# A decode block and its gradients: two more pools of big tiles, one at each end of SBUF, in place of an early, hurried middle of batch 1

## The chip, the core and the metric

The kernel runs on one NeuronCore of a Trainium2 chip. The metric is the device time of one execution in microseconds (us): before, 941.38 us, the median of three runs (940.76 to 941.86). The profile is of one execution whose span, from the first to the last instruction, is 938.9 us.

The engines are TensorE (PE in the profile, with its weight loads, PEld, apart), VectorE (DVE), ScalarE (ACT), GpSimd (POOL) and SyncE (SP). SP issues the loads, GpSimd the stores of the big gradients, ScalarE those of the weight gradients.

## The reference

One step of attention with a cache of keys and values, then a small ReLU network, and the gradients of all inputs:

```python
B, Sq, D = 2, 1, 640
H, Sk, Dh, Dff = 32, 4096, 128, 1728
q = layernorm(x) @ wq                        # B x H heads of 128
p = softmax(q . K * Dh**-0.5)                # K: [2, 32, 4096, 128] bf16
h = x + (p . V) @ wo                         # V: the same shape
h2 = h + relu(layernorm(h) @ w1) @ w2
out_0 = h2
out_1 .. out_7 = gradients for x, K, V, wq, wo, w1, w2 from grad_out
```

K and V of one head are 4096 x 128 bf16, 1 MB each; there are 64 pairs (batch, head). The gradients of K and V are as large as K and V and are outer products: for each head gV = p (x) go, and gK = gs (x) q, where go is the gradient of the head's output and gs = p * (V . go - p . (V . go)). So go has to be known first, and it needs the gradient that comes back through the network, w1 and wo: that is what the kernel calls the middle of a batch.

## The kernel before

**Pass one** walks over the 64 pairs: it loads K and V, transposes K, makes the scores, e = exp, the products K*e, and with them M = V^T (K*e) and the head's output. M (`MT`, one tile of 128 x 128 for each head) gives the gradient for q later, without a further pass over K. **Pass two** walks over the 64 pairs again, which it calls turns: it loads V once more (`W`), transposes it, makes V . go, and writes gV and gK. Turns 0 to 12 are laid between the iterations of pass one for batch 1; the others run by themselves when pass one has ended.

Between them lies the **middle** of a batch: wo, layer norm, w1, ReLU, the way back through w1, and go for each head by dot products of VectorE with rows of wo (`ttr`). It is a generator in the background queue `bg`. Three background queues are stepped, each by its own credit:

```python
def turn():                       # a dot product waits for a slot
    while slot[0] <= 0:
        yield 0.0
    slot[0] -= 1

def wait(n):                      # steps until another engine's result is due
    end = step[0] + n * spread[0]
    while step[0] < end and not forced[0]:
        yield 0.0
    yield

def middle_gen(b):
    ...                           # wo, layer norm, w1, ReLU
    for k in range(3):
        for c in range(ND):
            yield from turn()
            ttr(w1_t[:, c, k * FW:(k + 1) * FW], fbc[:, k * FW:(k + 1) * FW], gx2p[:, c, k:k + 1], FW)
            yield 0.85
    yield ("w1", b)
    ...                           # layer norm backward
    for h0, h1 in bounds:         # the kept heads first, then groups of 8
        yield from go_group(b, h0, h1, hbc)    # a ttr with wo for each head, then M's part; marks ("go", b, h)
```

**The big tiles.** K, V, W, the results gK and gV, the weights that are streamed, and the strips of the weight gradients share 12 tiles of 8 KB a partition (32 x 128 bf16). Each tile has a home under a tag: `ld` for loads, `g` for gK and gV, `f` for strips, `q` for weights late in the kernel. `take` gets a free tile of a tag, `give` returns it, and `share` says how many each tag ought to own; a tile moves over when it comes free. A tile that was handed on is written only when its last reader is done, and for gK and gV that is the store.

```python
NBIG = 12
homes = {"ld": list(range(NBIG)), "g": [], "f": [], "q": []}
def goes_to(tag):
    if owned[tag] > wanted.get(tag, NBIG):
        for other in homes:
            if owned[other] < wanted.get(other, 0):
                return other
    return tag
def more_home(tag, pool):
    homes[tag].append(len(pools)); pools.append(pool)
    free[tag] += 1; owned[tag] += 1
```

**Kept heads.** The V tiles of the last 6 heads of batch 0 and the last 5 of batch 1 are not given back after pass one, and are not loaded again. The order of the turns is

```python
KEPT = (6, 5)
turns = [(b, h) for b in range(B) for h in (*range(H - KEPT[b], H), *range(H - KEPT[b]))]
KEPT1_AT = 22
turns[KEPT1_AT:H + KEPT[1]] = turns[H:H + KEPT[1]] + turns[KEPT1_AT:H]
```

so the kept heads of batch 1 are turns 22 to 26, ahead of the last ten heads of batch 0.

**One turn of pass two** (half a tile is 128 x 2048; the lines L438, L451, L822 and so on of the profile are in these helpers):

```python
def p2_iter(j, busy):             # c = turn j, p = turn j - 1
    pair_matvec(p["dp"], p.pop("T3"), 3, gom[:, hp, bp, :, :])
    nc.vector.scalar_tensor_tensor(out=gsp[:], ...)          # gs of the turn before
    ...                                                      # go and q spread over the partitions, p in pairs
    c["T0"] = pair_transpose(c["W"], 0)
    gK = take("g", ...); outer_half(gK, p["rb"][:, 128:256], gsp, 0)
    yield
    outer_half(gK, p["rb"][:, 128:256], gsp, 1)
    nc.gpsimd.dma_start(out=natural(out_2, bp, hp), in_=gK[:]); give(gK)
    yield
    ...                                                      # T1; T2, with V . go of the quarters before
    c["T3"] = pair_transpose(c["W"], 3)
    give(c["W"], "g" if j < H and owned["g"] < 3 else None)
    gV = take("g", ...); outer_half(gV, c["rb"][:, 0:128], c["pp"], 0)
    yield
    outer_half(gV, c["rb"][:, 0:128], c["pp"], 1)
    nc.gpsimd.dma_start(out=natural(out_3, b, h), in_=gV[:]); give(gV)
    yield
```

**The late parts.** When w1 of batch 1 has been used, its memory is released and becomes a pool `fin` and one more big tile `big2`, of the tag `f`. `fin_gen` then makes the gradients of w2, w1, wo and wq (14.9 MB in 18 strips) with outer products of two rows on TensorE, copied from PSUM mostly by ScalarE; `outer_rows` takes a tile `f` for each strip once it has rested 13 steps. When every go is known, `gx_gen` loads wq again, transposes it and makes the gradient of x, and `mlp_out` makes h2 with w2.

The loop over the turns, after pass one:

```python
if i is None and plan[n - 1][0] is not None:     # the first turn that is alone
    share(ld=KEPT[1] + 3, g=4)
if fin is not None and not bg2 and not bg3:
    share(ld=7, g=6)
elif fin is not None and j >= KEPT1_AT + KEPT[1] - 1:
    share(ld=4, g=4, f=3, q=2)
...
if i is None:
    spread[0] = 2 if ("w1", B - 1) in done else 1
    hurry = ("go", *turns[KEPT1_AT]) not in done
    k = 0
    while g2 is not None:                        # seven steps a turn
        p2_step(); pump()
        slot[0] = int(k in ((0, 1, 3, 4, 5) if hurry else (1, 4)))
        k += 1
        bg_step(0, rate); bg_step(1, RATE2); bg_step(2, RATE3)
```

`pump` issues the next loads as long as a tile `ld` is free. `bg_until` forces the middle on if a turn's go isn't there yet.

Of the kernel before, what the change touches and what calls it, by code (L numbers as in the profile page):

```python
# [15 lines left out]
def kernel(  # L16
# [79 lines left out]

    def goes_to(tag):

        if owned[tag] > wanted.get(tag, NBIG):
            for other in homes:  # L100
                if owned[other] < wanted.get(other, 0):
                    return other
        return tag
# [218 lines left out]
    nc.vector.tensor_copy(out=gc[:].rearrange("p c b -> p b c"), in_=xg32[:, B:2 * B, :])  # L322
    run(ln_fwd(xg32[:, 0:B, :], B, x1c[:], rstd1[:]))

    wop = tc.alloc_tile_pool(name="wop", bufs=1)
    wts = tc.alloc_tile_pool(name="wts", bufs=1)
    wo_t = wop.tile([128, H, D], BF16)
    w1_t = wts.tile([128, ND, Dff], BF16)
    wo_r = A_wo.rearrange("(c p) d -> p c d", p=128)
# [62 lines left out]
    NP1 = len(pairs)  # L392
    KEPT = (6, 5)
    turns = [(b, h) for b in range(B) for h in (*range(H - KEPT[b], H), *range(H - KEPT[b]))]
    KEPT1_AT = 22
    turns[KEPT1_AT:H + KEPT[1]] = turns[H:H + KEPT[1]] + turns[KEPT1_AT:H]
    turn_of = {bh: j for j, bh in enumerate(turns)}
    kept = {(b, h) for b in range(B) for h in range(H - KEPT[b], H)}
    u_bank = [None]
# [64 lines left out]
    def p1_iter(i, dve_group, busy):  # L464
# [18 lines left out]

        def pk_tile(k):

            pk = mats.tile([128, HALF, 130], BF16, tag="pK", bufs=3, name="pk")
            nc.scalar.copy(out=pk[:, :, 128:129], in_=p["ep"][:, k * HALF:(k + 1) * HALF, 0:1])
            p["pk"].append(pk)

# [86 lines left out]
        if r is not None:  # L576
            br, hr = pairs[i - 2]
            m_part(7)
            if (br, hr) in kept:
                S2.setdefault(turn_of[(br, hr)], {})["W"] = r["V"]  # L580
            else:
                give(r["V"])
            MT = mats.tile([128, 128], BF16, tag="MT", bufs=NMT, name="MT")
            nc.scalar.copy(out=MT[:], in_=r["m"][:, 0:128])
            nc.scalar.copy(out=OU[:, br, hr:hr + 1], in_=r["m"][:, 128:129])
            MTs[(br, hr)] = MT
            del S1[i - 2]
# [109 lines left out]
    def mlp_out():  # L697

        ml32 = small.tile([128, ND, B], FP32, tag="ml32", bufs=1, name="ml32")
        nc.vector.memset(ml32[:], 0.0)  # L700
        for k in range(NW2):
            while free["q"] < 1:
                yield
            t = load_w2(k, "q", "(p c) d -> p c d")
            yield from wait(12)
            c1 = min(NF, (k + 1) * FP)
            m_ps = pst([128, ND, B], FP32, "mid", "mlp_ps")
            for c in range(ND):
                for cf in range(k * FP, c1):
                    kc = f_kc(cf)  # L710
                    nc.tensor.matmul(m_ps[:, c, :], lhsT=t[0:kc, cf - k * FP, c * 128:(c + 1) * 128],
                                     rhs=arow[0:kc, cf, :], start=(cf == k * FP), stop=(cf == c1 - 1))
            give(t)
            nc.vector.tensor_tensor(out=ml32[:], in0=m_ps[:], in1=ml32[:], op=ALU.add)
            yield
        ml_bf = small.tile([128, ND, B], BF16, tag="ml_bf", bufs=1, name="ml_bf")
        nc.vector.tensor_copy(out=ml_bf[:], in_=ml32[:])
        y_bf = small.tile([128, B, ND], BF16, tag="y_bf", bufs=1, name="y_bf")
        nc.vector.tensor_tensor(out=y_bf[:].rearrange("p b c -> p c b"), in0=h1c[:], in1=ml_bf[:], op=ALU.add)
        yield from wait(3)  # L720
        for b in range(B):
            store_row(y_bf[:, b, :], ND, out_0[b].rearrange("s (c p) -> (s c) p", p=128))
            yield

    def middle_gen(b):
# [69 lines left out]
        bounds += [(h, min(first, h + GH)) for h in range(0, first, GH)]  # L795
        for h0, h1 in bounds:
            yield from go_group(b, h0, h1, hbc)

    def ga_gen():

# [256 lines left out]
    M0_ITERS = 7  # L1057
    P2_AT = H + 2 + M0_ITERS
    RATES = (0.2, 0.8, 0.2, 0.8, 0.45)
    RATE2 = 0.58  # L1060
    RATE3 = 0.35
    plan = []
    i = j = 0
    while i <= NP1 + 1 or j <= NP1:
# [44 lines left out]
    pump()  # L1109
    q_piece(0)  # L1110
    pump()
    fin = big2 = None
    g2 = None

    MIXED = {1: 2, 3: 1, 4: 1, 6: 1}
# [9 lines left out]
    for n, (i, j) in enumerate(plan):  # L1125
        if i is not None and i % QP == 0 and 1 <= i // QP < NQ:
            q_piece(i // QP)
            pump()
        if i is None and plan[n - 1][0] is not None:
            share(ld=KEPT[1] + 3, g=4)  # L1130
        if fin is not None and not bg2 and not bg3:
            share(ld=7, g=6)
        elif fin is not None and j >= KEPT1_AT + KEPT[1] - 1:
            share(ld=4, g=4, f=3, q=2)
        if j is not None:
            while g2 is not None:
                p2_step()
# [3 lines left out]
        if i is None and ("w1", 1) in done and fin is None:  # L1141
# [3 lines left out]
            more_home("f", big2)  # L1145
            banks.update(sps=[2, 3], o=[4, 5, 6])
            bg2.append(("fin", fin_gen(fin)))
            bg3.append(("mlp", mlp_out()))
            bg3.append(("gx", gx_gen(fin)))
        late[0] = all(("go", B - 1, h) in done for h in range(H))  # L1150
        if i == 12:
            bg.append(("ga", ga_gen()))
        if i == H + 2:
# [5 lines left out]
        rate = RATES[0 if i is not None and i <= H + 1 else 1 if j is None and i < P2_AT else  # L1159
                     2 if i is not None else 3 if j <= H else 4]  # L1160
        if i is None:
            spread[0] = 2 if ("w1", B - 1) in done else 1
            hurry = ("go", *turns[KEPT1_AT]) not in done
            at_k[0] = 1
            k = 0
            while g2 is not None:
                p2_step()
                pump()
                slot[0] = int(k in ((0, 1, 3, 4, 5) if hurry else (1, 4)))
                k += 1  # L1170
                bg_step(0, rate)
                bg_step(1, RATE2)
                bg_step(2, RATE3)
# [28 lines left out]
        left = [q for q in left if q]  # L1202
    big2.release()
    fin.release()
    wop.release()


# [28 lines left out]
```

## Time and profile before

| what | value |
|---|---|
| time | 941.38 us (940.76 to 941.86) |
| span of the profiled run | 938.9 us |
| busy: PE, DVE, ACT, POOL | 767.6, 659.8, 551.1, 142.7 us |
| moved by DMA | 363.02 MB, mean 387 GB/s |
| of it the stores of gK and gV | 134.23 MB |
| last V load for pass one issued | 459 us |
| last gK store issued | 930.4 us |
| mean granted TensorE clock | 0.785 |

The page gives the busy time of each engine, the span in 40 slices with a tenth of busy share for each digit, the queues of the DMA, the chain of work that ended last, and groups of instructions: line, engine, what is written and read, the count, busy time and mean ns of one, and the idle time of the engine just before them with what ended it. A stretch of the table by stage gives, for each engine, busy us and the count of instructions, then the granted clock, the mean busy share of the 16 DMA engines and the rate. A share can read a little over 1. In the list of waits, `A <- B: x, n, y` says that A waited for B x us in all, n times, y us at the longest.

### The profile page before, as it was taken

The page shows a single profiled execution, that of the slowest core. Times are in us where ns is not written, and L with a number is a line of the kernel's source. Part 1 is how long each engine was busy: PE and PEld are TensorE (multiplying, and loading weights), DVE is VectorE, ACT ScalarE, POOL GpSimd, SP SyncE. Part 2 cuts the span into 40 slices and gives each one's busy share as a digit, 9 for nine tenths or more (in the row PEclk, how much of TensorE's full clock was granted, in tenths as well). Part 3 has the DMA queues.
Part 4 walks back from the last instruction along what each step waited for, and adds up shares of the span by engine and source line. Part 5 has one row for each costly group of instructions (what it writes and reads, how often), then busy time and mean ns, then how long its engine had stood idle before and what let it go on. Part 6 is the DMA issues. An engine that isn't in the chain of part 4 may idle for free.

```text
span 938.9 us, 26764 instructions
## 1 busy us (share of the span) xinstructions
PE 767.6 (82%) x11482; PEld 638.1 (68%) x11482; DVE 659.8 (70%) x1234; ACT 551.1 (59%) x1165; POOL 142.7 (15%) x249
## 2 busy tenths in 40 slices
PE   6999798999998888888868479877879858869962
PEld 5887687888787777777768367655666636747651
DVE  4655687866876887778667998877686454657656
ACT  4666566667775776667633356554654645756641
POOL 1222111121001101011011111111121111112112
PEclk9999999999998999989875755565555755765566
DMA  8999999997778999999988999999999999998998
GB/s 347 418 400 410 407 383 411 413 417 298 293 296 335 362 398 424 424 420 421 412 335 313 394 346 395 409 363 399 423 401 416 424 415 391 389 413 345 422 421 364
DMA packets 59478, 363.02 MB, mean 387 GB/s; under 512 B 5696, under 2 KB 15552, under 8 KB 19168
## 3 DMA queue, kind: packets, MB, share of 16 engines
q1 hardware_dynamic: 37920, 212.18, 57.7%
q0 software_dynamic: 18432, 134.23, 34.4%
q10 hardware_dynamic: 3008, 14.91, 3.9%
q8 instruction: 90, 1.47, 0.6%
q14 instruction: 28, 0.23, 0.1%
HBM read 212.16 MB, written 149.13 MB: 385 GB/s over the span
## 4 chain that ended last, share of the span: by engine, by line
PE 35%; DMA 34%; DVE 16%; ACT 9%; issue 4%; POOL 0%; SPq 0%; ACTq 0%; DVEq 0%; POOLq 0%
DMA out_dram<-gV 16%; DMA Kt<-in_A_k_cache_dram 15%; PE t_ps L438 7%; PE m_ps L472 7%; DVE gV L822 6%; PE t_ps L417 6%; ACT t_sb L422 5%; PE s_ps L428 3%; DVE gK L822 3%; PE o_ps L926 3%; DVE junk L651 3%; PE u_ps L497 2%; DMA out_dram<-gK 2%; DVE pk L479 2%; PE dp_ps L451 2%
## 5 line engine op out<-in xcount | busy, mean ns | idle before, releaser
L422 ACT COPY t_sb<-t_ps 128x1024 bf16<-128x1024 bf16 x223 | 216.5, 1012 | 46.3 <-PE t_ps L417 41.8
L443 ACT COPY t_sb<-t_ps 128x512 f32<-128x512 f32 x256 | 149.9, 588 | 156.8 <-PE t_ps L438 155.0
L438 PE MATMUL t_ps<-ident_f,Wt 128*128 128x128 f32 x848 | 197.7, 381 | 3.0 <-ACT t_sb L995 1.7
L472 PE MATMUL m_ps<-pk,Vt 128*128 128x129 bf16 x2048 | 191.7, 223 | 1.0 <-DVE pk L479 0.6
L479 DVE TENSOR_TENSOR pk<-Kt,ep 128x2048 bf16<-128x2048 bf16 x128 | 156.4, 1222 | 34.9 <-ACT ep L522 34.8
L822 DVE TENSOR_TENSOR gV<-rb,pp 128x2048 bf16<-128x2048 bf16 x128 | 153.6, 1219 | 36.9 <-DMA out_dram<-gV 34.6
L822 DVE TENSOR_TENSOR gK<-rb,gsp 128x2048 bf16<-128x2048 bf16 x128 | 152.6, 1224 | 32.8 <-DMA out_dram<-gK 21.0
L417 PE MATMUL t_ps<-ident_bf,Kt 128*128 128x128 bf16 x2048 | 153.5, 226 | 17.2 <-DMA Kt<-in_A_k_cache_dram 16.9
L438 PEld LDWEIGHTS t_ps<-ident_f,Wt 128*128 128x128 f32 x848 | 136.7, 198 | 25.3 <-issue 14.8
L472 PEld LDWEIGHTS <-Vt 128*128 128x128 bf16 x2048 | 128.9, 99 | 29.0 <-issue 29.0
L417 PEld LDWEIGHTS <-Kt 128*128 128x128 bf16 x2048 | 126.4, 101 | 20.0 <-DMA Kt<-in_A_k_cache_dram 19.8
L451 PEld LDWEIGHTS <-t_sb 128*128 128x128 bf16 x2048 | 96.6, 107 | 55.1 <-issue 28.0
L428 PE MATMUL s_ps<-qc,t_sb 128*128 128x1 bf16 x2048 | 88.9, 164 | 19.0 <-ACT t_sb L422 17.6
L451 PE MATMUL dp_ps<-gom,t_sb 128*128 128x2 bf16 x2048 | 95.6, 168 | 9.7 <-ACT t_sb L443 8.9
L428 PEld LDWEIGHTS <-t_sb 128*128 128x128 bf16 x2048 | 75.1, 97 | 31.6 <-ACT t_sb L422 28.3
L879 POOL DMA_DIRECT2D out_dram<-gV x64 | 34.3, 536 | 295.3 <-DVE gV L822 203.8
L568 POOL COPY P_bf<-ep 128x32 bf16<-128x32 bf16 x40 | 42.3, 1059 | 219.2 <-ACT ep L522 219.2
L860 POOL DMA_DIRECT2D out_dram<-gK x64 | 34.1, 533 | 272.7 <-DVE gK L822 213.7
L935 ACT CAST ot<-o_ps 128x512 bf16<-128x512 f32 (+4 forms) x137 | 61.1, 477 | 6.1 <-PE o_ps L926 2.4
L849 ACT ACTIVATE rb<-dp_ps,rt 128x256 bf16<-128x256 f32 x64 | 30.6, 478 | 41.9 <-PE dp_ps L844 40.7
L563 DVE TENSOR_REDUCE rmax<-s_ps 128x1 bf16<-128x32 f32 x64 | 12.3, 192 | 59.6 <-PE s_ps L428 59.5
L651 DVE CUSTOM_DVE_ANT_0 junk<-wo_t,hbc 128x640 bf16<-128x640 bf16 x64 | 52.4, 818 | 0.1
(194 smaller groups left out, 802.9 us busy)
## 6 DMA issues: line engine op xcount, KB each, us to landing
Kt<-in_A_k_cache_dram SPq DMA_DIRECT2D x64, 1024.0 KB, 14.5
Vt<-in_A_v_cache_dram SPq DMA_DIRECT2D x64, 1024.0 KB, 12.3
out_dram<-gV POOLq DMA_DIRECT2D x64, 1024.0 KB, 10.6
out_dram<-gK POOLq DMA_DIRECT2D x64, 1024.0 KB, 10.5
Wt<-in_A_v_cache_dram SPq DMA_DIRECT2D x53, 1024.0 KB, 10.9
wo_t<-in_A_wo_dram SPq DMA_DIRECT2D x4, 1280.0 KB, 16.4
wqs<-in_A_wq_dram SPq DMA_DIRECT2D x5, 1024.0 KB, 11.6
wq_t<-in_A_wq_dram SPq DMA_DIRECT2D x5, 960.0 KB, 5.6
```

The costliest lines, as they stand in the source:

```text
L417: nc.tensor.transpose(t_ps[:, j, :], nat[:, g * GT + j, :], ident_bf[:])
L422: nc.scalar.copy(out=t_sb[:], in_=t_ps[:])
L428: nc.tensor.matmul(dst[:, sc:sc + 1], lhsT=t_sb[:, j, :], rhs=vec, start=True, stop=True)
L438: nc.tensor.transpose(t_ps[:, j, :], natf[:, 2 * cc:2 * cc + 2, :].rearrange("p c k -> p (c k)"), ident_f[:])
L443: nc.scalar.copy(out=t_sb[:], in_=t_ps[:])
L451: nc.tensor.matmul(dst[:, sc:sc + 2], lhsT=v[:, j, :, par], rhs=vecs[:, par, :], start=(par == 0), stop=(par == 1))
L472: nc.tensor.matmul(r["m"][:, 0:129], lhsT=r["V"][:, sc, :], rhs=r["pk"][sc // HALF][:, sc % HALF, 0:129], start=(sc == 0), stop=(sc == NSC ...
L479: nc.vector.tensor_tensor(out=p["pk"][k][:, :, 0:128].rearrange("p s (a two) -> p s a two", two=2), in0=p["K"][:, sl, :].rearrange("p s (a ...
L568: (nc.gpsimd if i < P2_AT else nc.vector).tensor_copy(out=P_bf[:, bhp, :], in_=ep[:, :, 0])
L651: nc.vector.tensor_tensor_reduce(out=junk[0:kc, 0:width], in0=in0, in1=in1, scale=1.0, scalar=0.0, op0=ALU.mult, op1=ALU.add, accum_out=acc)
L822: nc.vector.tensor_tensor(out=pairs_view(dst[:, sl, :]), in0=row.rearrange("p (a two) -> p a two", two=2)[:, None, :, :].to_broadcast([128 ...
L935: nc.scalar.copy(out=ot[0:P, k, n0:n0 + nn], in_=o_ps[0:P, 0:nn])
```

## The change

It gives back one thing and adds another.

Given back: batch 1's middle isn't hurried any more. The kept heads of batch 1 are turns 32 to 36 again, `spread` is 2 for the whole stage, and there are three slots a turn for the dot products until turn 32 and two after, in place of five until the kept heads' go is known.

Added: memory that has done its work becomes big tiles. The pools lie as two stacks, from both ends of SBUF, so that each can be released without the other: pK (the K*e buffers, three of 4,160 bytes a partition) is the top of one, w1 and, below it, wo with the 44 tiles M (40,960 and 11,264 bytes a partition) are the other. When pass one ends, pK becomes one more big tile, `big1`. When the last go is known, wo and M become six more, `big3`. The number of big tiles so goes from 12 to 13, to 14 with `big2`, and to 20; before, it was 12 and 13.

With them go: `mlp_out` is put at the end of the middle of batch 1 (queue `bg`) rather than in `bg3` ahead of `gx_gen`; its sum is issued one step after its matmuls; the rates of the two late queues are raised (0.58 to 0.65 and 0.35 to 0.45); and `share` gives the new tiles to the tags.

```diff
-        if owned[tag] > wanted.get(tag, NBIG):
+        if owned[tag] > wanted.get(tag, len(pools)):
...
-    wop = tc.alloc_tile_pool(name="wop", bufs=1)
-    wts = tc.alloc_tile_pool(name="wts", bufs=1)
+    wop = tc.alloc_tile_pool(name="wop", bufs=1, side="right")
+    wts = tc.alloc_tile_pool(name="wts", bufs=1, side="right")
+    pkp = tc.alloc_tile_pool(name="pkp", bufs=1)
...
-    KEPT1_AT = 22
-    turns[KEPT1_AT:H + KEPT[1]] = turns[H:H + KEPT[1]] + turns[KEPT1_AT:H]
...
-            pk = mats.tile([128, HALF, 130], BF16, tag="pK", bufs=3, name="pk")
+            pk = pkp.tile([128, HALF, 130], BF16, tag="pK", bufs=3, name="pk")
...
-            MT = mats.tile([128, 128], BF16, tag="MT", bufs=NMT, name="MT")
+            MT = wop.tile([128, 128], BF16, tag="MT", bufs=NMT, name="MT")
...
             give(t)
+            yield
             nc.vector.tensor_tensor(out=ml32[:], in0=m_ps[:], in1=ml32[:], op=ALU.add)
-            yield
...
             yield from go_group(b, h0, h1, hbc)
+        if b > 0:
+            yield from mlp_out()
...
-    RATE2 = 0.58
-    RATE3 = 0.35
+    RATE2 = 0.65
+    RATE3 = 0.45
...
+        all_go = all(("go", B - 1, h) in done for h in range(H))
         if i is None and plan[n - 1][0] is not None:
-            share(ld=KEPT[1] + 3, g=4)
+            pkp.release()
+            big1 = tc.alloc_tile_pool(name="big1", bufs=1)
+            more_home("ld", big1)
+            share(ld=KEPT[1] + 4, g=4)
+        if all_go and not late[0]:
+            wop.release()
+            big3 = tc.alloc_tile_pool(name="big3", bufs=1, side="right")
+            for tag in ("ld", "ld", "g", "g", "f", "q"):
+                more_home(tag, big3)
+        late[0] = all_go
+        more = int(late[0])
         if fin is not None and not bg2 and not bg3:
-            share(ld=7, g=6)
-        elif fin is not None and j >= KEPT1_AT + KEPT[1] - 1:
-            share(ld=4, g=4, f=3, q=2)
+            share(ld=8 + 3 * more, g=6 + 3 * more)
+        elif fin is not None and j >= H + KEPT[1] - 1:
+            share(ld=5 + 2 * more, g=4 + 2 * more, f=3 + more, q=2 + more)
...
-            bg3.append(("mlp", mlp_out()))
...
-            spread[0] = 2 if ("w1", B - 1) in done else 1
-            hurry = ("go", *turns[KEPT1_AT]) not in done
+            spread[0] = 2
...
-                slot[0] = int(k in ((0, 1, 3, 4, 5) if hurry else (1, 4)))
+                slot[0] = int(k in ((1, 3, 5) if j <= H else (1, 4)))
```

More of the change, by code (lines that the diff above doesn't have):

```diff
@@ L1111 @@
     pump()
-    fin = big2 = None
+    fin = big1 = big2 = big3 = None
     g2 = None
@@ L1147 @@
             bg2.append(("fin", fin_gen(fin)))
-            bg3.append(("mlp", mlp_out()))
             bg3.append(("gx", gx_gen(fin)))
-        late[0] = all(("go", B - 1, h) in done for h in range(H))
         if i == 12:
@@ L1204 @@
     fin.release()
-    wop.release()
+    big1.release()
+    big3.release()
 _INS = ['A_x', 'A_k_cache', 'A_v_cache', 'A_wq', 'A_wo', 'B_x', 'B_w1', 'B_w2', 'grad_out']
```

## The prediction

> **What bounds the kernel now.** I read the 40 slices of the page first: the rows of the DMA engines' busy share and of the bytes moved, under the granted TensorE clock.
>
> ```profile
> PEclk9999999999998999989875755565555755765566
> DMA  8999999997778999999988999999999999998998
> GB/s 347 418 400 410 407 383 411 413 417 298 293 296 335 362 398 424 424 420 421 412 335 313 394 346 395 409 363 399 423 401 416 424 415 391 389 413 345 422 421 364
> ```
>
> A slice is 23.5 us. Most read 9, and the best move 424 GB/s, so the DMA engines are the bound nearly everywhere. There are two dents. One lies at slices 9 to 12 (220 to 320 us), where the middle of batch 0 runs inside the first pass; the change touches nothing there. The other lies at slices 20 to 23 (470 to 560 us), where the first pass ends and the middle of batch 1 is hurried. From slice 20 on TensorE has about half its clock. Next I cut the second half in stretches of 20 us; the columns are the busy time of PE, weight loads, VectorE (DVE), ScalarE and GpSimd with their instructions, the clock, the DMA share, GB/s.
>
> ```profile
> 460.00:480.00 20.00, 18.61 (x297) 16.84 (x298) 14.40 (x25) 11.07 (x25) 1.85 (x4) 0.84 0.83 306
> 480.00:500.00 20.00, 11.63 (x153) 10.51 (x151) 13.23 (x39) 5.86 (x13) 2.24 (x6) 0.66 0.87 365
> 500.00:520.00 20.00, 18.52 (x262) 17.19 (x259) 14.68 (x25) 8.71 (x16) 3.93 (x7) 0.57 0.91 341
> 520.00:540.00 20.00, 7.26 (x100) 5.80 (x101) 19.76 (x41) 5.88 (x12) 3.40 (x8) 0.69 0.99 399
> 540.00:560.00 20.00, 15.24 (x151) 13.43 (x151) 18.16 (x36) 10.23 (x23) 3.14 (x7) 0.50 0.89 333
> ...
> 840.00:860.00 20.00, 17.76 (x138) 11.33 (x137) 11.67 (x19) 10.88 (x20) 1.84 (x4) 0.50 0.85 320
> ...
> 900.00:920.00 20.00, 13.69 (x167) 11.96 (x167) 14.47 (x15) 9.50 (x18) 4.49 (x8) 0.75 1.01 421
> 920.00:940.00 20.00, 1.71 (x32) 1.29 (x29) 10.04 (x11) 1.17 (x2) 3.39 (x6) 0.59 0.79 330
> ```
>
> The stretches from 560 to 840 and from 860 to 920, not shown, all have a share of 0.99 to 1.02. Only those shown have DMA time to give back. The chain that ended last and the groups of pass two then say what the stores cost VectorE.
>
> ```profile
> PE 35%; DMA 34%; DVE 16%; ACT 9%; issue 4%; POOL 0%; SPq 0%; ACTq 0%; DVEq 0%; POOLq 0%
> ...
> L822 DVE TENSOR_TENSOR gV<-rb,pp 128x2048 bf16<-128x2048 bf16 x128 | 153.6, 1219 | 36.9 <-DMA out_dram<-gV 34.6
> L822 DVE TENSOR_TENSOR gK<-rb,gsp 128x2048 bf16<-128x2048 bf16 x128 | 152.6, 1224 | 32.8 <-DMA out_dram<-gK 21.0
> ...
> L651 DVE CUSTOM_DVE_ANT_0 junk<-wo_t,hbc 128x640 bf16<-128x640 bf16 x64 | 52.4, 818 | 0.1
> ```
>
> VectorE stood still some 67 us because a result tile's store had not landed (34.6 + 21.0, and 10.1 and 1.4 crosswise in the full list of groups). That is a lack of tiles, but wherever the DMA share is 1.0 the wait only shows that the queue is full. One such wait falls in the dent: the list of waits of 460 to 500 us has
>
> ```profile
> DVE gK L822 <- DMA out_dram<-gV: 4.3, 1, 4.3
> ```
>
> and TensorE, in its own order, then waited 5.6 us for an OFc that VectorE was to make behind that gK.
>
> **What the Trainium skill says.** "DMA: Bandwidth & Descriptors", Specifications, gives 435 GB/s as the fabric's ceiling; the best stretches here show 424 to 425, so those slices can't be much improved. The same page, "Issuing engines are not separate DMA queues", says that the SP, ScalarE and GpSimd queues run on the same 16 engines; the trace agrees, with V loads, gK/gV stores and weight gradients sharing 395 to 425 GB/s at a share of 1.0. "Perfetto Trace Analysis", Optimization Strategy, says that a repeated gap on the engine that should be saturated can mean that there is no room for the next tile. In the dent that fits the 4.3 us; after 560 us the saturated engines show no gap, so there it gives no reason to hope. "SBUF — State Buffer", "SBUF: two separate sides", has engine and DMA ports disjoint, so which end of the memory a pool lies at should cost nothing; no run here shows that yet.
>
> **The change part by part.** All of pass one up to its last iteration issues the same work; pK and MT only lie in other pools. I put 0 us on the first 470 us.
>
> *One more tile at the end of pass one.* Before, 12 tiles: 5 hold kept V tiles of batch 1, 3 then 4 are for results, 3 are left for V loads. After, 13: `ld` 9 and `g` 4, so 4 for loads, and since the new tile is free at once the fourth `g` tile is there at once. That should take most of the 4.3 us wait at 482 us, and starts V loads earlier. (By the table of DMA issues a load takes 10.9 us to land, and a turn is about 8, so three tiles in rotation leave little slack.)
>
> *No hurry.* Per turn of pass two VectorE has four half-tile products, 4 x 1.22 = 4.88, and gsp, 0.28: 5.16 us. A dot product of the middle is 0.75 (w1) or 0.82 (wo) plus 0.08 to read it, some 0.85. Hurried: five a turn, 5.16 + 4.2 = 9.4 us. After: three a turn up to turn 32, 5.16 + 2.5 = 7.7, with small pieces 8.0. The DMA engines need 3 x 1.049 MB for a turn, at 0.42 MB/us 7.5 us. So the hurried turns were bound by VectorE by almost 2 us and the new ones by about 0.5. The timeline of GpSimd's stores bears the sum out: from turn 12's gV store at 481.9 to turn 20's at 555.7 are 73.8 us for eight turns, 9.2 each.
>
> *What is to be had.* Saturation reads 1.01. Lost: (0.18 + 0.14 + 0.10 + 0.02 + 0.12) x 20 = 11.2 us in 460 to 560, and 0.16 x 20 = 3.2 us in 840 to 860. The last 8.5 us, from issue of the last gK store at 930.4 to the end, are mostly one landing; perhaps 1 to 2 us is there. Ceiling: about 16 us. In the dent I take back 60%, because the layer norm's chain still alternates VectorE and TensorE and three dots a turn are still slightly over the DMA time: -6.7 us.
>
> *Kept heads back at turns 32 to 36.* They need no load, so a turn moves 2.1 MB rather than 3.1 wherever it lies; the loads run ahead into freed tiles. The bytes are conserved: 0 us. But the five tiles stay tied up ten turns longer, which uses up the new tile until then: no gain in turns 22 to 36 beyond the dent.
>
> *Weight gradients start later.* Fin, the part of the kernel that makes them, starts when w1 is finished: before, at 538 us, in turn 18. After: 15 dots take 5 turns rather than 3 and the doubled waits cost about 2 more, so turn 22 or 23, and it has one `f` tile until turn 36 (before: until 26). Then 0.65 instead of 0.58 credits a step catches up: the 30 turns from the third store (620 us) to the last (896 us) become 27. That ends it around turn 61 of 63; before, it was 59. The wq part, 716 to 876 us, starts about turn 45 and ends near 59. The bytes are the same, the DMA time is the same; what it may cost is TensorE at half clock: PE is busy 17 to 19 of 20 in many stretches, and turns 45 to 60 now hold more of its work. I put +2 us on it.
>
> *Six more tiles when the last go is known.* At about turn 45 the tiles go from 14 to 20. At a DMA share of 1.0 they move nothing; what they can do is to bridge holes like 840 to 860 (10 us of TensorE and ScalarE work without a store) because three more loads and results are in flight: -2 us. At the end more stores lie ready: -1.5 us.
>
> Sum: -6.7 + 2 - 2 - 1.5 = -8.2; 941.4 - 8.2 = **933 us**.
>
> **The rivals.** (a) *All of the slack comes back*: 4 tiles end the starvation at 480 us, the dents fill, and the span falls by 14 to 16 us: about 926. For it: every lost stretch has a lack of tiles or too much VectorE work in it, and the change treats both. Against it: PE was busy 18.5 of 20 in 500 to 520 at a clock of 0.57, which no tile changes. (b) *The tail pays*: fin, mlp and wq, delayed by four or more turns, crowd the last twenty. TensorE and ScalarE then bind at half clock, the last chunks come after the last turn, and the span rises to 945 to 952. For it: the hole at 840 to 860 is of that kind already. Against it: 20 tiles decouple the stores, and the rates are raised. (c) *Nothing*: what is saved at 480 us is given back by later starts, because DMA time is conserved and the kept tiles stay in memory; 938 to 942. (d) A gain over 19 us would need the saturated stretches to move more bytes a microsecond. The 375 to 400 GB/s of some of them come with fin's smaller packets, which stay; I see no way.
>
> **Range and chances.** 933 lies between (a), which I give 30%, and (c) with 25%; my middle case takes 30%, (b) 12%, (d) 3%. The range of 8 in 10 runs from 923, somewhat better than (a), to 946, into (b). Two per cent is 18.8 us: faster needs under 922.6, more than the ceiling I count, but the count of 1.01 as full is rough: 0.10. Slower needs over 960.2: 0.04. Within: 0.86.
>
> **What would show it.** Right, if 0 to 460 us look alike; the shares of 480 to 560 rise to 0.95 or more with VectorE below 18 of 20; VectorE's wait for the store at 482 us shrinks; the first store of a weight gradient moves from 579 to 600 us or later; and 860 to the end stays at 1.0. Wrong, if the dent stays although VectorE has less to do (then the chain or TensorE set it), if the last `ot` store comes after the last gK store, if a hole over 10 us opens after 700 us with TensorE busy through it, or if loads wait in turns 22 to 36 for tiles.

## The result and the profile after

The changed kernel takes 930.07 us (median of four runs, 928.68 to 931.83), the kernel before 941.62 us beside it: a ratio of 0.9872, 95% interval 0.9843 to 0.9901. The span of the profiled run is 926.8 us, where it was 938.9.

The rows by slice, the chain's engines and the two groups of results in the page of the changed kernel (a slice is now 23.2 us, and the line of `outer_half` is L823):

```profile
PEclk9999999999999999999995775756555557556766
DMA  8999999997787999999999999999999999999998
GB/s 346 418 400 408 406 386 410 411 416 286 300 334 280 358 390 423 423 422 422 418 362 394 389 424 403 397 410 395 391 418 391 426 425 424 425 385 369 417 420 345
...
PE 38%; DMA 32%; DVE 13%; ACT 10%; issue 5%; POOL 0%; SPq 0%; POOLq 0%; ACTq 0%; DVEq 0%
...
L823 DVE TENSOR_TENSOR gK<-rb,gsp 128x2048 bf16<-128x2048 bf16 x128 | 152.4, 1226 | 25.4 <-DMA out_dram<-gK 12.6
...
L823 DVE TENSOR_TENSOR gV<-rb,pp 128x2048 bf16<-128x2048 bf16 x128 | 152.7, 1218 | 20.3 <-DMA out_dram<-gV 15.1
```

The dent at slices 9 to 12 is still there; it is batch 0's, which the change leaves alone. The second dent is gone: slices 20 to 23 read 362 394 389 424 GB/s where they read 335 313 394 346. VectorE's idle time ahead of gK and gV fell from 32.8 and 36.9 us to 25.4 and 20.3. The stretches of 20 us of the changed kernel, with the columns as before:

```profile
460.00:480.00 20.00, 17.32 (x315) 15.18 (x313) 17.29 (x36) 10.99 (x28) 2.00 (x4) 1.00 0.93 351
480.00:500.00 20.00, 12.34 (x146) 11.15 (x144) 13.55 (x31) 6.38 (x14) 2.61 (x6) 0.63 1.01 397
500.00:520.00 20.00, 16.27 (x240) 15.52 (x239) 12.94 (x28) 6.10 (x11) 3.39 (x8) 0.50 1.01 415
520.00:540.00 20.00, 16.93 (x248) 14.17 (x247) 18.64 (x27) 14.38 (x28) 3.23 (x8) 0.93 1.00 384
540.00:560.00 20.00, 5.05 (x72) 3.93 (x70) 15.30 (x26) 4.27 (x8) 3.29 (x8) 0.67 1.01 425
...
820.00:840.00 20.00, 17.08 (x175) 14.60 (x175) 11.08 (x25) 10.39 (x24) 3.05 (x5) 0.50 0.93 356
840.00:860.00 20.00, 18.16 (x166) 12.18 (x166) 17.65 (x24) 15.21 (x31) 4.47 (x9) 0.67 0.97 385
...
900.00:920.00 20.00, 6.19 (x97) 4.96 (x95) 12.19 (x13) 5.27 (x10) 4.74 (x8) 0.71 1.01 414
920.00:940.00 20.00, 0.00 (x0) 0.00 (x0) 0.00 (x0) 0.00 (x0) 0.00 (x0) 0.78 0.15 62
```

From 480 to 560 the DMA share is full, with VectorE at 12.9 to 18.6 of 20. Two small holes are left at 820 and 840, and after them the DMA engines work at a full share to 920 us. The last store is issued at 913.5 us, and the span ends when it lands, 13 us later; before, the last gK store was issued at 930.4 and the span ended 8.5 us later.

To set runs side by side I add up, over the stretches from 460 to 920, what the DMA share lacks of 1.01 (a full stretch), times 20 us. It is worked out from one profile of each kernel, while the medians are of several runs. The table itself shows how far it can be trusted: the changed kernel, x3, x5, x6 and x12 issue the same work until about 700 us, when the last go is known, and they read 0.8 to 2.8 in the column of 460 to 560 and 0.8 to 3.0 in the next one. A difference of 2 us in a column says nothing. From 460 to 480 us this is plainest: the kernel before and x10 issue the same instructions there, and their shares are 0.83 and 0.99.

| kernel | median us | ratio, 95% interval | lost 460-560 | 560-720 | 720-920 |
|---|---|---|---|---|---|
| before | 941.6 to 942.8 | 1 | 11.2 | 1.0 | 3.8 |
| changed | 930.1 | 0.9872 (0.9843-0.9901) | 1.8 | 0.8 | 2.4 |
| x1 calm, no new tile | 939.5 | 0.9980 (0.9960-0.9999) | 3.4 | 2.4 | 5.4 |
| x2 without the first tile | 931.7 | 0.9903 (0.9880-0.9925) | 1.6 | 4.0 | 0.6 |
| x3 without the six | 937.9 | 0.9956 (0.9937-0.9976) | 0.8 | 3.0 | 4.6 |
| x4 all tiles, hurried | 941.5 | 1.0013 (0.9992-1.0033) | 8.4 | 3.8 | 3.6 |
| x5 one late tile, q | 936.7 | 0.9948 (0.9930-0.9965) | 2.8 | 2.2 | 6.4 |
| x6 four late tiles, ld and g | 936.5 | 0.9944 (0.9915-0.9973) | 2.4 | 1.8 | 6.8 |
| x7 before, short dots | 937.6 | 0.9958 (0.9933-0.9982) | 9.2 | 0.4 | 5.2 |
| x8 first tile used first | 931.5 | 0.9896 (0.9862-0.9930) | 2.4 | 1.2 | 2.0 |
| x9 changed, short dots | 930.5 | 0.9882 (0.9848-0.9916) | 3.4 | 4.0 | 2.2 |
| x10 before, long waits | 943.0 | 1.0001 (0.9978-1.0024) | 5.2 | 8.8 | 1.6 |
| x12 five late tiles, no f | 928.7 | 0.9863 (0.9832-0.9894) | 1.2 | 3.0 | 2.0 |
| x13 six V tiles kept | 932.2 | 0.9893 (0.9862-0.9923) | 1.8 | 7.4 | 2.8 |

The ratios are to the kernel before on the same chip, and they decide. Each interval is the range in which the ratio lies with 95% confidence.

### The profile page after: what moved, and what is told of

Read it like the earlier page. It is cut to its first block, busy times and chain, and to the rows that moved or that the text cites. A ratio compares the mean times of both kernels' runs of the same rounds, so it can differ in the third digit from the quotient of the medians.

```text
span 926.8 us, 26767 instructions
## 1 busy us (share of the span) xinstructions
PE 757.0 (82%) x11482; PEld 636.1 (69%) x11482; DVE 662.1 (71%) x1237; ACT 549.1 (59%) x1162; POOL 146.0 (16%) x249
## 4 chain that ended last, share of the span: by engine, by line
PE 38%; DMA 32%; DVE 13%; ACT 10%; issue 5%; POOL 0%; SPq 0%; POOLq 0%; ACTq 0%; DVEq 0%
DMA Kt<-in_A_k_cache_dram 13%; DMA out_dram<-gV 9%; DMA out_dram<-gK 8%; PE m_ps L471 7%; PE t_ps L437 7%; PE t_ps L416 7%; ACT t_sb L421 5%; DVE gV L823 4%; PE s_ps L427 4%; DMA wqs<-in_A_wq_dram 3%; PE o_ps L927 3%; DVE gK L823 3%; PE u_ps L496 2%; ACT t_sb L442 2%; DVE pk L478 2%
## 5 line engine op out<-in xcount | busy, mean ns | idle before, releaser
L437 PE MATMUL t_ps<-ident_f,Wt 128*128 128x128 f32 x848 | 191.7, 373 | 1.2 <-ACT t_sb L421 1.0
L823 DVE TENSOR_TENSOR gK<-rb,gsp 128x2048 bf16<-128x2048 bf16 x128 | 152.4, 1226 | 25.4 <-DMA out_dram<-gK 12.6
L823 DVE TENSOR_TENSOR gV<-rb,pp 128x2048 bf16<-128x2048 bf16 x128 | 152.7, 1218 | 20.3 <-DMA out_dram<-gV 15.1
L437 PEld LDWEIGHTS t_ps<-ident_f,Wt 128*128 128x128 f32 x848 | 133.7, 194 | 24.6 <-issue 17.4
L450 PEld LDWEIGHTS <-t_sb 128*128 128x128 bf16 x2048 | 95.5, 106 | 37.5 <-ACT t_sb L442 18.4
L583 ACT CAST MT<-m_ps 128x128 bf16<-128x128 f32 x64 | 17.0, 266 | 58.7 <-PE m_ps L471 58.7
```

Of the source, the lines that this page charges most:

```text
L437: nc.tensor.transpose(t_ps[:, j, :], natf[:, 2 * cc:2 * cc + 2, :].rearrange("p c k -> p (c k)"), ident_f[:])
L450: nc.tensor.matmul(dst[:, sc:sc + 2], lhsT=v[:, j, :, par], rhs=vecs[:, par, :], start=(par == 0), stop=(par == 1))
L823: nc.vector.tensor_tensor(out=pairs_view(dst[:, sl, :]), in0=row.rearrange("p (a two) -> p a two", two=2)[:, None, :, :].to_broadcast([128 ...
```

## The experiments

"Calm" below is the middle of batch 1 as in the changed kernel: `spread` 2, three slots a turn, kept heads at turns 32 to 36.

### x1: calm, no new tile

```diff
-            big1 = tc.alloc_tile_pool(name="big1", bufs=1)
-            more_home("ld", big1)
-            share(ld=KEPT[1] + 4, g=4)
+            share(ld=KEPT[1] + 3, g=4)
...
-            wop.release()
-            big3 = tc.alloc_tile_pool(name="big3", bufs=1, side="right")
-            for tag in ("ld", "ld", "g", "g", "f", "q"):
-                more_home(tag, big3)
...
-        more = int(late[0])
+        more = 0
...                          # and one ld less in both later calls of share
```

> The changed kernel without any of the seven new tiles: the calm middle, the late kept heads and the new rates alone (12 big tiles, then 13). Theory 'calm': the gain comes from VectorE no longer being asked for five dot products a turn; then 930 to 934 us, with the DMA share at 0.95 or more from 500 to 560. Theory 'tiles': the gain comes from the room; then 939 to 943 us, with the share below 0.93 in 460 to 500 and holes later.

Measured: 939.5 us. The stretches of x1:

```profile
480.00:500.00 20.00, 13.95 (x180) 12.26 (x177) 14.53 (x28) 7.07 (x15) 3.15 (x7) 0.74 0.98 392
500.00:520.00 20.00, 14.86 (x255) 13.88 (x253) 14.25 (x33) 6.01 (x12) 3.88 (x9) 0.64 0.99 395
...
800.00:820.00 20.00, 16.64 (x133) 12.15 (x131) 10.27 (x12) 10.65 (x20) 1.85 (x4) 0.50 0.92 332
820.00:840.00 20.00, 17.48 (x210) 15.41 (x209) 12.14 (x17) 12.99 (x29) 3.10 (x6) 0.58 0.99 388
840.00:860.00 20.00, 17.39 (x152) 11.99 (x149) 10.98 (x14) 13.03 (x24) 2.62 (x6) 0.59 1.01 423
860.00:880.00 20.00, 15.27 (x147) 10.73 (x145) 9.73 (x15) 10.95 (x21) 2.09 (x5) 0.50 0.85 308
```

Both theories are half right. The dent is gone without any tile: 0.98 and 0.99 where the kernel before has 0.87 and 0.91. But little of it arrives at the end: 0.2% in the ratio, hardly clear of the noise. Late there are two holes, 0.92 at 800 and 0.85 at 860, where the kernel before has one, 0.85 at 840. By the table 7.8 us were won at the dent and 3.0 given back later, which is not far above the scatter of the table; pass one was 2.3 us behind in this profile (turn 12's gV store at 484.1 us, not 481.9), and some 3 us more show in no share. So the late holes account for a part of the missing gain, and the rest stays open.

### x4: all the tiles, hurried

```diff
+    KEPT1_AT = 22
+    turns[KEPT1_AT:H + KEPT[1]] = turns[H:H + KEPT[1]] + turns[KEPT1_AT:H]
...
-        elif fin is not None and j >= H + KEPT[1] - 1:
+        elif fin is not None and j >= KEPT1_AT + KEPT[1] - 1:
...
-            spread[0] = 2
+            spread[0] = 2 if ("w1", B - 1) in done else 1
+            hurry = ("go", *turns[KEPT1_AT]) not in done
...
-                slot[0] = int(k in ((1, 3, 5) if j <= H else (1, 4)))
+                slot[0] = int(k in ((0, 1, 3, 4, 5) if hurry else (1, 4)))
```

> The changed kernel with the hurried middle back (five dot products a turn, short waits, kept heads at turns 22 to 26) and all seven new tiles. Theory 'calm': the VectorE-bound turns are back, 937 to 942 us, with VectorE at 18 to 20 of 20 us and a DMA share of 0.9 to 0.95 somewhere in 500 to 560. Theory 'tiles': 928 to 932 us, like the changed kernel or better, since the weight gradients start earlier too.

Measured: 941.5 us, nothing gained with all seven tiles. Its stretches:

```profile
480.00:500.00 20.00, 12.81 (x162) 11.68 (x159) 13.35 (x34) 6.42 (x13) 2.61 (x6) 0.67 1.00 404
500.00:520.00 20.00, 17.80 (x257) 16.83 (x257) 14.44 (x28) 6.81 (x13) 3.92 (x7) 0.50 0.89 342
...
540.00:560.00 20.00, 13.82 (x135) 12.50 (x135) 18.03 (x38) 9.68 (x22) 3.38 (x8) 0.50 0.88 327
...
680.00:700.00 20.00, 16.47 (x133) 11.85 (x134) 13.79 (x27) 10.47 (x24) 3.14 (x7) 0.50 0.88 333
...
820.00:840.00 20.00, 15.90 (x123) 9.79 (x122) 11.37 (x24) 9.98 (x19) 2.08 (x5) 0.50 0.83 316
```

Only the stretch at 480 is mended (1.00 for 0.87); 500 and 540 stay as they were, 680 has a new hole, and the late one lies at 820 (0.83) rather than at 840 (0.85). Cut in fives, the hole of the kernel before is at 495 and 500 us (0.53 and 0.63), and that of x4 at 500 alone (1.00 and 0.62): the tiles shorten it, but with the short waits they don't close it. So tiles without calm are worth nothing that shows, calm without tiles is worth 0.2%, and both together 1.3%: they aren't two gains that add up. The moved `mlp_out` and the two raised rates are in x1 as in x4, so alone they bring no more than these runs do; no run takes them out of the changed kernel.

### x2 and x3: without the first tile, without the six

x2 takes the first three lines of x1's edit with their replacement, and the one ld less in the later calls; x3 takes the rest.

> The changed kernel without the tile made of the K*e buffers; the six late tiles stay. Theory 'calm': 930 to 932 us. Theory 'tiles', with the first tile as the one that counts: 935 to 940 us, and the DMA share in 480 to 500 falls from 1.01 to about 0.9.

> The changed kernel without the six late tiles; the first one stays. My estimate of them was -2 us for the hole late in the kernel and -1.5 us at the end, so 933 to 934 us. If the DMA queue is full anyway in the last 200 us they are worth nothing: 929 to 931. If the later weight gradients need them: 936 or more, with a DMA share below 0.95 between 720 and 880.

Measured: x2 931.7 us, x3 937.9 us. The first tile is worth at most a little (0.9903 against 0.9872, with intervals that overlap), and the share from 480 to 500 in x2 is 0.99. The six late tiles are what counts: 0.9956 against 0.9872, with intervals apart, some 8 us. I had expected 3 to 4. (Of these 8 the profiles show a part: x3's span is 931.2 us, 4.4 above the changed kernel's, and 3.4 us more of DMA time are lost.) The hole of x3, and the line that the tile view of `gx_ps` gives for the matmuls of the gradient of x:

```profile
860.00:880.00 20.00, 16.39 (x160) 13.78 (x160) 13.67 (x24) 12.29 (x25) 2.62 (x6) 0.50 0.83 291
```

```profile
L1004 PE MATMUL gx_ps<-GQc,t_sb x160: 163/165/211, 731.5 to 870.4; 128*128 128x2 bf16 x160
```

and the same line of the changed kernel:

```profile
L1004 PE MATMUL gx_ps<-GQc,t_sb x160: 163/165/211, 732.4 to 827.9; 128*128 128x2 bf16 x160
```

The gradient of x begins at the same time in both and ends 42 us later without the tiles. The strips of wq's gradient begin at 834 us in x3 (842 in the changed kernel). So in x3 both lie in the same turns, and by its chain from 840 to 882 us the path runs almost wholly through TensorE and ScalarE, which pass PSUM to and fro:

```profile
by line: PE t_ps L437 30.9%; PE o_ps L927 19.6%; PE t_ps L994 11.3%; PE dp_ps L450 5.6%; ACT t_sb L442 5.6%; ACT ot L936 4.7%; PE rw_ps L898 4.5%; ACT t_sb L996 4.5%; PE gx_ps L1004 4.4%; issue 2.8%; PE dp_ps L845 1.7%; DVE ot L934 1.6%; DV
```

No step of it is a DMA, and VectorE has a few per cent. That gave a new theory, the overlap of these two jobs at half clock, against plain room for loads and results.

### x5, x6 and x12: which of the six

```diff
-            for tag in ("ld", "ld", "g", "g", "f", "q"):
+            for tag in ("q",):                          # x5
+            for tag in ("ld", "ld", "g", "g"):          # x6
+            for tag in ("ld", "ld", "g", "g", "q"):     # x12
...                          # share asks for as many as there are
```

> The changed kernel with one late tile in place of six, of the tag q, so that one more piece of wq can be on its way while the gradient of x is made. New theory 'overlap': without the six tiles the gradient of x lasted until 870 us and ran into the strips of wq's gradient, both on TensorE and ScalarE; what the tiles buy is that it ends ahead of them. Then this one tile gives nearly all: 930 to 933 us, the last gx matmul before 840 us. Theory 'room': loads and results in flight bridge the holes; then 936 to 938 us.

> The changed kernel with four late tiles, two for V loads and two for gK and gV, none for q and f. 'Overlap': little of the gain, 935 to 938 us, the last gx matmul near 870 us, a stretch with a DMA share below 0.9 there. 'Room': 930 to 933 us, no such stretch, whenever the gradient of x ends.

Measured: x5 936.7 us, x6 936.5 us. In x5 the gradient of x ends at 832 us, as the overlap theory had it, and still the time is that of x3. In x6 it ends at 874 us and the time is that of x3 too. The stretches of x5, then those of x6:

```profile
800.00:820.00 20.00, 17.46 (x156) 12.97 (x156) 8.04 (x11) 11.67 (x23) 1.56 (x5) 0.50 0.90 360
820.00:840.00 20.00, 16.52 (x161) 13.17 (x160) 10.59 (x19) 10.11 (x23) 3.42 (x6) 0.50 0.87 338
840.00:860.00 20.00, 18.79 (x179) 14.27 (x180) 16.50 (x27) 14.25 (x31) 3.85 (x8) 0.67 0.96 364
```

```profile
800.00:820.00 20.00, 16.32 (x136) 11.89 (x135) 9.71 (x11) 10.65 (x20) 1.83 (x4) 0.50 1.01 423
...
840.00:860.00 20.00, 17.71 (x142) 11.43 (x142) 9.26 (x11) 11.49 (x20) 2.61 (x6) 0.55 1.01 423
860.00:880.00 20.00, 15.33 (x148) 12.04 (x147) 11.72 (x22) 11.55 (x22) 1.31 (x3) 0.50 0.94 354
880.00:900.00 20.00, 17.69 (x136) 11.88 (x136) 13.34 (x19) 11.88 (x24) 3.93 (x9) 0.50 0.84 342
900.00:920.00 20.00, 17.92 (x165) 13.64 (x163) 16.90 (x19) 12.29 (x24) 4.79 (x9) 0.57 0.91 368
```

x5 has its hole at 800 to 860, most of it while the gradient of x is still being made. x6 is full in that stretch (1.01 throughout) and has its hole at 860 to 920. There the strips of wq's gradient run from 838 to 908 us and the gradient of x until 874, so the two do meet, but the share is 1.01 at first and lowest, 0.84, when the gradient of x has ended. A reading that fits both: in x5 no loads and results are in store to bridge the early hole, and in x6 what is in store lasts for 20 us of the meeting and is then used up. No run shows this step by step. What the times show is that neither the one tile nor the room brings the gain alone.

> The changed kernel with five of the six late tiles: two for loads, two for results, one for wq, none for the strips of the weight gradients. If it takes both an early end of the gradient of x (the q tile) and room in flight (the other four), which each alone gave about 1 us: 930 to 932 us, the last gx matmul before 835 us, no stretch with a DMA share below 0.92 between 720 and 900. If the strips' tile is what counts: 935 to 938 us.

Measured: 928.7 us, ratio 0.9863: all of the six tiles' gain with five. The last gx matmul is at 830 us, and no stretch from 720 to 900 is below 0.95; the two lowest are

```profile
820.00:840.00 20.00, 17.07 (x166) 14.37 (x164) 10.02 (x20) 10.24 (x22) 3.05 (x5) 0.50 0.95 371
840.00:860.00 20.00, 18.17 (x179) 12.49 (x177) 17.54 (x29) 14.89 (x32) 4.48 (x9) 0.67 0.96 368
```

The strips' tile `f` is worth nothing that shows.

### x7 and x10: what made the dent

x7 is the kernel before with the dot products of batch 1's middle over an eighth of their columns; it leaves seven eighths of those sums out, and everything else runs in the same order.

```diff
+                w = FW if b == 0 else FW // 8
-                ttr(w1_t[:, c, k * FW:(k + 1) * FW], fbc[:, k * FW:(k + 1) * FW], gx2p[:, c, k:k + 1], FW)
+                ttr(w1_t[:, c, k * FW:k * FW + w], fbc[:, k * FW:k * FW + w], gx2p[:, c, k:k + 1], w)
...
+            w = D if b == 0 else D // 8
-            ttr(wo_t[:, h0 + k, :], hbc[:], go32[:, k:k + 1], D)
+            ttr(wo_t[:, h0 + k, 0:w], hbc[:, 0:w], go32[:, k:k + 1], w)
```

> The kernel before, with the dot products of batch 1's middle over an eighth of their columns (it leaves seven eighths of these sums out): 15 of 576 and 32 of 640 columns. Same order, same waits, same slots; VectorE is freed of about 0.55 us a dot, some 26 us in all. If VectorE's load made the dent at 480 to 560 us: the DMA share there is 0.97 or more, 928 to 935 us. If the order of the chain (the layer norm between VectorE and TensorE with short waits) made it: the share stays below 0.93 and the time at 938 to 942. If the late overlap decides, the dent goes but the time falls by 4 us at most.

Measured: 937.6 us, and these stretches:

```profile
480.00:500.00 20.00, 12.33 (x153) 11.20 (x151) 13.03 (x35) 6.42 (x13) 2.61 (x6) 0.62 0.90 370
500.00:520.00 20.00, 17.82 (x259) 16.57 (x258) 14.46 (x32) 7.32 (x14) 3.92 (x7) 0.53 0.86 312
520.00:540.00 20.00, 9.29 (x120) 7.45 (x121) 13.88 (x39) 7.27 (x14) 4.02 (x8) 0.73 1.01 404
540.00:560.00 20.00, 14.80 (x178) 12.76 (x177) 18.09 (x42) 11.23 (x27) 3.77 (x9) 0.67 0.97 365
```

The ratio is 0.9958: taking some 26 us of VectorE's work away brings some 4 us of time in the kernel before. The part at 540 is mended (0.97 for 0.89); that one was VectorE's load. The part from 480 to 520 is as before (0.90 and 0.86). It can't have been the dots: in the kernel before the first of them starts at 515 us. x10 changes only the waits of the kernel before:

```diff
-            spread[0] = 2 if ("w1", B - 1) in done else 1
+            spread[0] = 2
```

> The kernel before with one value changed: the steps that batch 1's middle waits between engines are doubled from the start of the stage (as in the changed kernel), while it keeps five slots a turn for the dot products and the kept heads at turns 22 to 26. If the short waits made the first part of the dent, from 480 to 520 us (there no dot product runs yet): the DMA share there is 0.97 or more instead of 0.87 and 0.91, and the part from 540 to 560 stays near 0.9; 937 to 940 us. If the first part came from something else (the tile, the order of the turns): the share stays at 0.9 and the time at 941.

Measured: 943.0 us, with

```profile
480.00:500.00 20.00, 13.45 (x171) 12.25 (x169) 14.64 (x33) 7.01 (x14) 3.15 (x7) 0.61 0.96 401
500.00:520.00 20.00, 17.57 (x253) 16.55 (x252) 14.35 (x29) 6.72 (x13) 3.88 (x8) 0.50 0.99 376
520.00:540.00 20.00, 13.07 (x202) 11.36 (x200) 17.50 (x30) 11.39 (x22) 3.16 (x7) 0.93 1.01 413
540.00:560.00 20.00, 6.27 (x53) 5.48 (x52) 17.56 (x35) 4.11 (x8) 3.88 (x8) 0.50 0.84 335
560.00:580.00 20.00, 12.81 (x142) 11.15 (x142) 18.21 (x39) 9.44 (x23) 2.32 (x4) 0.59 0.71 272
```

The first part is mended by the longer waits alone: 0.96 and 0.99. How the short waits make the hole is not shown step by step: in the kernel before VectorE waits 3.9 us for `ar_ps` and TensorE 2.1 us for `x2c`, but the changed kernel has a wait of 3.7 us in that chain as well. The timelines of VectorE and of the stores suggest one way; first the kernel before, then x10:

```profile
496.39 1.23 DVE L822 TENSOR_TENSOR gK<-rb,gsp 128x2048 bf16<-128x2048 bf16 x1
499.35 1.22 DVE L822 TENSOR_TENSOR gK<-rb,gsp 128x2048 bf16<-128x2048 bf16 x1
500.86 0.53 POOL L860 DMA_DIRECT2D out_dram<-gK  x1 [4.45 <-DVE gK L822]
```

```profile
495.13 2.36 DVE L822 TENSOR_TENSOR gK<-rb,gsp 128x2048 bf16<-128x2048 bf16 x2
497.79 0.53 POOL L860 DMA_DIRECT2D out_dram<-gK  x1 [2.74 <-DVE gK L822]
```

With the short waits, nine small steps of the layer norm stand on VectorE between the two halves of a gK, and its store goes out 5.2 us after the one before it. With the long waits the halves follow each other, and the store goes out after 3.5 us. What x10 shows is that the waits' length decides. But now the middle is late for turn 22, whose go it has to bring: it is forced, the time is above the 937 to 940 expected, and a hole of 0.84 and 0.71 follows. The list of waits from 545 to 580 us names it:

```profile
PE dp_ps L844 <- DVE gsp L835: 15.4, 1, 15.4
```

All of TensorE's work for the next turns stood behind that one wait. No gV or gK store was issued between 558.4 and 570.3 us. So the longer waits and the later kept heads belong together: longer waits are free only if the turn that needs the result comes later. The three slots in place of five have no run of their own.

### x8: the new tile taken first

```diff
-            more_home("ld", big1)
+            more_home("g", big1)
+            homes["g"].insert(0, homes["g"].pop())
```

> The changed kernel with the tile made of the K*e buffers put at the head of the free results' tiles rather than at the end of a list. If the first wait of VectorE for a store (5.2 us at 481 us) is there because tiles are taken in the order in which they were given back, it goes, TensorE's wait for OFc with it, and the middle starts 4 to 5 us earlier; the span falls by 0 to 3 us, since the DMA share is 1.0 at that time already: 927 to 930 us. If the wait is one for any tile of the four, nothing changes: 930 us and 5 us of wait.

Measured: 931.5 us, ratio 0.9896, no different from the changed kernel within the intervals. In the changed kernel the wait I had counted on was still there, even longer than before (from its list of waits, 460 to 500 us):

```profile
DVE gK L823 <- DMA out_dram<-gV: 5.2, 1, 5.2
```

In x8 that line is gone from the list; a wait of gV for 2.6 us is left. TensorE's wait for OFc falls from 6.5 to 1.4 us, and OFc is made 3.9 us earlier. So the wait came from the order in which tiles are taken, the oldest first, and it cost nothing that shows: the DMA share at that time is 1.01 with it and without it.

### x9: is VectorE still a bound after the change?

x9 is the edit of x7 on the changed kernel.

> The changed kernel with the dot products of batch 1's middle over an eighth of their columns (seven eighths of these sums are left out), which frees VectorE of some 26 us. If the changed kernel is bound by the DMA engines in that stage: 928 to 931 us, within 2 us of the changed kernel. If three dots a turn still bind VectorE: 920 to 926 us.

Measured: 930.5 us, ratio 0.9882, against 0.9872. Taking some 26 us of VectorE's work away, with seven eighths of those sums left out, brings nothing that shows, so three dots a turn don't set the time. In the kernel before, the same edit brought 4 us (x7).

### x13: one more V tile kept

```diff
-    KEPT = (6, 5)
+    KEPT = (6, 6)
...
-            share(ld=KEPT[1] + 4, g=4)
+            share(ld=9, g=4)
```

> The changed kernel with six V tiles of batch 1 kept rather than five: 1.05 MB less to load, and one tile less for other loads until turn 32. If bytes are what is left to save: 1.05 MB at 0.42 MB a us is 2.5 us, so 927 to 929 us. If the loads need the tile: 930 to 936 us, with a DMA share below 0.97 between 480 and 640.

Measured: 932.2 us, ratio 0.9893. The 1.05 MB saved don't show. I had looked for the price between 480 and 640; the share is full there, and the holes come a little later:

```profile
640.00:660.00 20.00, 12.89 (x104) 9.96 (x101) 15.50 (x26) 8.65 (x20) 2.62 (x6) 0.50 0.87 324
...
680.00:700.00 20.00, 11.06 (x126) 8.37 (x125) 15.99 (x28) 8.30 (x17) 5.03 (x8) 0.67 0.86 355
```

Its time is within the intervals of the changed kernel, so what is clear is only that the saved bytes bought nothing. The two holes are deeper than the scatter: in the same stretches the changed kernel, x3, x5, x6 and x12 read 0.95 or more. With one tile fewer for loads they fit the second expectation; x2, which lacks a tile at that time too, reads 0.91 and 0.96. No run shows that the tile is their cause.

## Why the prediction was right, point by point

The forecast of 933 us, with 923 to 946, stands against 930.07. The sum was right for partly wrong terms, and that is in part luck: by the ratios the calm middle and its later gradients are together worth 2 us (x1) to 4 us (x3, with the first tile), where I had 4.7, and the six tiles some 8 us, where I had 3.5.

**The bound and the ceiling.** Right. What the kernel could gain was what the DMA share lacked: 16 us by my count, and 11.0 of them came back (16.0 lost before, 5.0 after), with 11.5 us off the median. So close an agreement is chance, for 2 us of it lie between 460 and 480 us, where the share scatters by itself. The full stretches moved 375 to 425 GB/s, not 395 to 425 as I wrote (600 to 620 us: share 1.00, 375 GB/s). Nothing came from the stretches that were full already, and x9, which frees VectorE, is no faster.

**The end of pass one.** I said that the fourth tile for results would take away VectorE's 4.3 us at 482 us. Wrong: the wait is 5.2 us after the change. It did no harm that shows (x8). The tile itself is worth no more than the intervals hide (x2).

**No hurry.** I gave it 60% of the dent, -6.7 us, by counting five dots a turn against three. Nearly all of the dent came back: from 480 to 560 us 7.6 us were lost before and 0.2 after. The account by VectorE's load holds for 540 to 560 us only (x7). The larger part, 480 to 520, has no dots in it; it goes with the short waits of the chain (x10), and in x4, with the tiles and the short waits, about half of it is left. I had named that chain, but as what would stay in the way, not as what the change loosens: it doubles the waits, and I booked that under a later start of the weight gradients only. The 9.2 us a turn that seemed to bear out my 9.4 did so by chance. Turns 16 to 18, which hold all fifteen dots with w1, took 8.0, 8.4 and 8.4 us from one gV store to the next; turns 13 and 15, with 13.7 and 10.6 us, raised the mean and have no dots. I had added durations that overlap in the timeline: from one gsp to the next, 522.1 to 530.5 us, VectorE works without a gap, and its durations add up to 9.3 us in these 8.4.

**Kept heads back at turns 32 to 36.** I wrote 0 us because the bytes are the same. By itself that is not what the order is for: it moves the turn that needs the middle's result. x10 shows what the longer waits cost with the early turn, 943.0 us.

**Later weight gradients, +2, and six tiles, -3.5.** The direction was right, and both sizes were too small. With calm alone (x1) most of the gain at 480 us doesn't reach the end; 7.8 us of DMA time are lost after 560 us, for 4.8 before, which is a part of it. That is what rival (b) feared, "the tail pays". The six tiles are worth some 8 us (x3), as a tool to keep that from happening and not as a gain of their own (x4). The dates were close: w1 was done in turn 22 (predicted 22 or 23), and the last strip was issued at 895.1 us, in turn 61 (predicted 61). The gradient of x was stored by 852 us, in turn 55 rather than 59; I had not counted that the q tile lets its loads run ahead.

**The end.** I gave 1.5 us, and nothing of it shows. The last stores queue for 13 us after the last issue, for 8.5 before: more of them lay ready, as I had said. But what the end costs is the time in which the DMA engines run dry, and that is no shorter. Before, their share is 1.01 until 935 and 0.18 in the 3.9 us that are left; after, it is 1.01 until 920, 0.59 from 920 to 925, and 0 in the last 1.8 us. By the same count as above, 3.2 us are lost there before and 3.9 after.

**The signs.** The shares of 480 to 560 us rose to 1.00 and more, and 860 to 920 stayed full. Two signs missed a little: VectorE is at 18.6 of 20 from 520 to 540 us, where I wanted less than 18 and the share is full all the same, and the first store of a weight gradient goes out at 594 us, not at 600 or later. The pools' new places cost nothing that shows: turn 12's gV store is issued at 481.3 us, for 481.9 before.

**Rivals.** (a) was nearest in time, for another reason than it gave: not the one tile at 480 us. (c) is what x1 does: 939.5 us against its 938 to 942. (d) did not come: the best stretches of 20 us move 426 GB/s, for 425 before.

## What to carry to other kernels

When transfers bound a kernel, add up what their busy share lacks in each stretch: that is the ceiling, and an edit that mends one stretch has gained nothing until the later ones are seen to hold. A chain of small steps that alternates between two engines cost less here with longer waits than with shorter ones, as long as the work that needs its end was moved back too; where such a chain runs between large pieces of work, both lengths are worth a run. Buffers that are worth nothing in one order of work can be what makes another order pay, so try the two together and apart.

## What was not expected of the hardware

A wait of VectorE for a store's landing, 5.2 us with TensorE 6.5 us idle behind it, cost nothing that shows (x8): the DMA share was 1.01 from 480 to 500 us, with the wait and without it. TensorE's granted clock lay between 0.5 and 0.76 in all of the stretches from 560 to 920 us, before and after, and at 0.5 in half of them or more. In these stretches the gradient of x took 114 us before (737 to 852), 95.5 us in the changed kernel and 139 us in x3. Among the calm variants the difference goes with the q tile: with it the gradient of x took 95 us in x5 too, without it 138 us in x6. In x3, where it met the strips of wq's gradient, the DMA share fell to 0.83.
